# Wave 0's loads on one queue, and the weight queue asked later, in a fused attention and MLP kernel

## The chip, the cores and the metric

The kernel runs on one core of a Trainium2 chip. The core has five engines that work side by side and meet at semaphores: TensorE (PE in the profile; its weight loads are PEld), VectorE (DVE), ScalarE (ACT), GpSimd (POOL) and SyncE (SP). Transfers between memory and the core's SBUF are done by 16 DMA engines. An instruction on SP or POOL asks for a transfer; SP's transfers and POOL's are told apart in the profile as queue q1 (hardware_dynamic) and queue q0 (software_dynamic). The metric is device time in microseconds (us) for one launch, as the median of several runs.

## The reference

Four batches of eight heads, 768 tokens, head size 64. A linear attention with decay runs over blocks of 64 tokens, and its output goes through a two-layer MLP of 512 to 2048 to 512 features:

```python
for b in range(nb):
    qb, kb, vb = (q[:, :, sl], k[:, :, sl], v[:, :, sl])
    intra = np.einsum('bhic,bhjc->bhij', qb, kb) * Dmask[None]
    intra = np.einsum('bhij,bhjd->bhid', intra, vb)
    inter = np.einsum('bhid,bhde->bhie', qb * lam_pow[None], kv_state)
    out[:, :, sl] = intra + inter
    kv_state = lam_block * kv_state + np.einsum('bhsd,bhse->bhde', kb * rev_pow[None], vb)
...
h = x @ w_in
g = h * (1.0 / (1.0 + np.exp(-1.702 * h)))
return g @ w_out
```

All inputs and the output are float32. The kernel multiplies in bfloat16 and sums in float32.

## The kernel before

**Waves.** The tokens are cut into six waves (`NW`) of 128 positions in each of the four batches, 512 columns in all. Each wave goes through the attention (scores, masks, output, state), then through the MLP, and leaves 512 rows of output. The first two waves (`ND` = 2) are laid out in pairs: q, k and v of two tokens of a batch pair stand beside each other, `c` = 0 or 1 is the batch, and each `load_one` of wave 0 or 1 brings one tensor for one c: 512 KB. Wave 0 asks for it in two halves of 256 KB (four heads each), so that the first cast can start early. In the text q1, k1 and v1 are the tensors of c = 1, q0, k0 and v0 those of c = 0.

**What is done with a load.** `do_cast` (L193) multiplies k or q by a power of the decay and writes bfloat16; `g` = 0 or 1 is one half of the heads, two instructions each. `turn_pe` (L232) transposes on PE through the identity and copies back to SBUF. `d_scores` (L251) makes the scores on PE and masks them on DVE (with `split` the second half goes through an ACT copy first). `cast_v` (L223) writes v as bfloat16 in two instructions, one for each of the two interleaved tokens, and its argument says which engine takes which. `d_one` and `d_state` make the state (tile `ps_kv`), `d_out` the output (tile `ps_o`), `d_x` moves it into the MLP's input `xT`. `mlp1_half` (L406) and `mlp1` (L396) multiply by `w_in`.

**Weights.** `w_in` comes in five chunks of 2, 3, 4, 4 and 3 feature blocks of 128 (256, 384, 512, 512 and 384 KB as bfloat16), `w_out` in four chunks of 512 KB. All nine are asked on GpSimd's queue, because they are turned from float32 to bfloat16 on the way. `load_w_in(j)` and `load_w_out(j)` each issue one transfer.

**Order.** Every engine runs its instructions in the order of the program text, written out by hand under `tc.manual_schedule()`. Before it, `load(0)` asks SP for k0, q0, v0, k1 and q1, in ten halves. v1 isn't among them: GpSimd asks for it in one piece, behind `w_in` chunk 0. GpSimd's order around the change is: a copy of one element of q0's second half, which holds the engine until that half has landed (`gate_pool`, L654); `w_in` 0; v1; the cast of k1's first half; `w_in` 1; the cast of k1's second half; `w_in` 2 to 4; `w_out` 0 to 3; a mask for later waves. `gate_sync` (L637) holds SP in the same way until `w_out` 1 has landed, and then wave 1's k, q and v are asked (`load(1)`).

PE's order in wave 0's attention is: transposes of k0 and q0, scores of c = 0, state, the first half of the k1 transposes, output of c = 0, state, q1 first half, k1 second half, q1 second half, scores of c = 1, the first MLP half (`w_in` 0), state and output of c = 1, and then the rest of the MLP's first layer (`w_in` 1 to 4).

For wave 1, GpSimd casts v0 and then k1, PE transposes that k1 and goes on with the output of c = 0 (`end(1, 0)`).

Of the kernel before, what the change touches and what calls it, by code (L numbers as in the profile page):

```python
# [25 lines left out]
def kernel(  # L26
# [13 lines left out]
    nc = tc.nc  # L40
    f32 = mybir.dt.float32
    bf16 = mybir.dt.bfloat16
    B, H, S, D = q.shape
# [33 lines left out]
    loaded = {}  # L77

    def load_one(w, c, nm, src):
        x = ld.tile([P, H, 2 * D], f32, tag=f"{nm}{c}", bufs=LD_BUFS[nm], name=f"{nm}f")  # L80
        if w < ND:
            n = H if w or (nm == "v" and c) else H // 2
            for h in range(0, H, n):
                (nc.gpsimd if w == 0 and c and nm == "v" else nc.sync).dma_start(  # L84
                    out=x[:, h : h + n],
                    in_=src[2 * w + c, h : h + n, 0 : 2 * P, :].rearrange("h (s a) d -> s h (a d)", a=2))
        else:
            nc.sync.dma_start(out=x.rearrange("p h (a d) -> p (h a) d", a=2),
                              in_=src[2 * c : 2 * c + 2, :, w * P : (w + 1) * P, :].rearrange("b h s d -> s (b h) d"))
        loaded[w, c, nm] = x  # L90

    def load(w, nms="kqv"):
        src = {"k": k, "q": q, "v": v}
        if w < ND:
            for c in range(HF):
                for nm in nms:
                    if w or c == 0 or nm != "v":
                        load_one(w, c, nm, src[nm])
        else:
            for nm in nms:  # L100
                for c in range(HF):
                    load_one(w, c, nm, src[nm])
# [3 lines left out]
    ones = const.tile([1, P], f32)  # L106
    nc.vector.memset(ones, 1.0)
    load(0)

    nc.scalar.preload_act_table_set("natural_log_exp_and_others")  # L110
# [32 lines left out]
    def fill(n, new=None):  # L143
        if new:
            fill_ps[0] = acc("ps_fill", shape=[P, W], tag=new)
        for _ in range(n):
            nc.tensor.matmul(fill_ps[0], zero[:, 0:P], zero, start=True, stop=True)
# [25 lines left out]
    NCH = FFC // CW  # L173
    IN_CH = [2, 3, 4, 4, 3]
# [4 lines left out]
    def load_w_in(j):  # L179
        c0 = sum(IN_CH[:j]) * P  # L180
        nc.gpsimd.dma_start(
            out=w_in_sb[j], in_=moe_w_in.rearrange("(kc ki) f -> ki kc f", ki=P)[:, :, c0 : c0 + IN_CH[j] * P])

    def load_w_out(j):
        nc.gpsimd.dma_start(
            out=w_out_sb[j], in_=moe_w_out.rearrange("(fc fi) d -> fi fc d", fi=P)[:, j * CW : (j + 1) * CW, :])
# [6 lines left out]
    def do_cast(w, c, nm, eng, g=None):  # L193
        if g in (None, 0):
            cast[w, c, nm] = work.tile([P, 2, HD], bf16, tag=f"{nm}s{c}", bufs={"k": 2, "q": 1}[nm], name=f"{nm}s")
        f, x = loaded[w, c, nm], cast[w, c, nm]
        if w < ND:
            pw = {"k": kd_pow, "q": qd_pow}[nm]
            for R in (0, 1) if g is None else (g,):
                for j in range(2):  # L200
                    h = slice(4 * R + 2 * j, 4 * R + 2 * j + 2)
                    eng.tensor_tensor(x.rearrange("p a (r i j d) -> p r j i a d", i=2, j=2, d=D)[:, R, j],
                                      f[:, h].rearrange("p i (a d) -> p i a d", a=2),
                                      pw[:, h].unsqueeze(3).to_broadcast([P, 2, 2, D]), op=MUL)
        else:
            pw = {"k": k_pow, "q": q_pow}[nm]
            n = 2 * H // 4
            for j in range(2):
                eng.tensor_tensor(x.rearrange("p b (r i j d) -> p j (b r) i d", i=2, j=2, d=D)[:, j],  # L209
                                  f.rearrange("p h (a d) -> p (h a) d", a=2).rearrange("p (n j i) d -> p j n i d", j=2, i=2)[:, j],  # L210
                                  pw.rearrange("p b (r j i) -> p j (b r) i", i=2, j=2)[:, j].unsqueeze(3).to_broadcast([P, n, 2, D]),
                                  op=MUL)
# [10 lines left out]
    def cast_v(w, c, copies=(pool_copy, pool_copy)):  # L223
        f = loaded.pop((w, c, "v"))
        dst = v_sb[w % 2]
        if w < ND:
            for a in range(2):
                copies[a](dst[:, 2 * c + a], f.rearrange("p h (a d) -> p h a d", a=2)[:, :, a, :])
        else:
            copies[0](dst[:, 2 * c : 2 * c + 2].rearrange("p b h d -> p (b h d)"), f.rearrange("p h e -> p (h e)"))  # L230
# [20 lines left out]
    def d_scores(w, c, pp, split=False):  # L251
        kT = trans[w, c, "k"]
        s2 = [acc("ps_s") for _ in range(2)]
        for i in range(2):
            r = 2 * pp + i
            for a in range(2):
                for blk, bs in enumerate((A, Z)):
                    for h, hs in enumerate((A, Z)):
                        nc.tensor.matmul(s2[h][bs, 2 * i + a, :], kT[hs, 2 * r + a, bs], q_of(w, c, hs, r, blk),
                                         start=True, stop=True)  # L260
        for h in range(2):
            sm = work.tile([P, 2, 2, P], bf16, tag="sm", bufs=8, name="sm")
            flat = s2[h].rearrange("p (i a) s -> p i (a s)", i=2)
            if split and h:
                nc.scalar.copy(sm.rearrange("p i a s -> p i (a s)"), flat)
                flat = sm.rearrange("p i a s -> p i (a s)")
            nc.vector.tensor_tensor(sm.rearrange("p i a s -> p i (a s)"), flat,  # L267
                                    mask_d.rearrange("p o a b s -> p o (a b s)").to_broadcast([P, 2, 2 * P]), op=MUL)
            masked[w, c, pp, h] = sm
# [14 lines left out]
    def d_one(w, c, tag="a"):  # L284
        states[w, c] = t = acc("ps_kv", shape=[P, NP, D], tag=tag)
        d_state(w, c, t, A)
# [278 lines left out]
    def one_step(w, s):  # L565
# [18 lines left out]
        elif s[0] in "kq":  # L584
            do_cast(x, int(a), s[0], nc.vector)
        elif s[0] in "KQ":
            do_cast(x, int(a), s[0].lower(), nc.gpsimd)
        elif s[0] == "t":
            turn_dma(x, int(s[2]), s[1])
        elif s[0] == "v":  # L590
            cast_v(x, int(s[1]), ((act_copy, dve_copy)[s[2:] == "v"],))
        elif s[0] == "S":
            n_scores(x, int(a))
        elif s[0] == "M":
            n_masks(x, int(a))
        elif s[0] == "m":
            n_masks(x, int(a), True)
        elif s[0] == "R":
            n_rest(x)
        elif s[0] == "o":  # L600
            c11.pop(w)()
        elif s[0] == "X":
            x_sums(x)
        elif s[0] == "G":
            gate_pool(x_sum[w][3][0:1, 0, 0:1])
        elif s[0] == "g":
            m0, m1 = {"l": (0, 4), "h": (4, 8)}[s[1]]
            g_sums(w, m0, m1, tuple(int(c) - 1 for c in s[2:]))
        elif s[0] == "L":
            load(w + (1 if a == "w" else 2), "kq" if a == "k" else "v")  # L610
        else:
            raise ValueError(s)
# [20 lines left out]
    def gate_pool(x):  # L633
        nc.gpsimd.tensor_copy(behind_q, x)  # L634
# [4 lines left out]
    with tc.manual_schedule():  # L639
# [8 lines left out]
        for nm, copies in (("k", (dve_copy, act_copy)), ("q", (act_copy, dve_copy))):  # L648
            for g in range(2):
                do_cast(0, 0, nm, nc.vector, g)  # L650
            for g in range(2):
                turn_pe(0, 0, nm, copies[g], g)
                fill(2 - g if nm == "k" else 1 - g)
        gate_pool(loaded[0, 0, "q"][0:1, H // 2, 0:1])  # L654
        load_w_in(0)
        load_one(0, 1, "v", v)
        cast_v(0, 0, (act_copy, act_copy))
        d_scores(0, 0, 0)
        d_scores(0, 0, 1)
        fill(3)  # L660
        do_cast(0, 1, "k", nc.gpsimd, 0)
        load_w_in(1)
        do_cast(0, 1, "k", nc.gpsimd, 1)
        for j in range(2, len(IN_CH)):
            load_w_in(j)
        for j in range(NCH):
            load_w_out(j)
        d_one(0, 0, "mm")
        d_keep(0, 0)
        turn_pe(0, 1, "k", act_copy, 0)  # L670
# [10 lines left out]
        d_x(0, 0, 1, oz, act_copy)  # L681
        fill(1, "a")
        d_scores(0, 1, 0, True)
        cast_v(0, 1, (act_copy, dve_copy))
        nc.gpsimd.affine_select(mask, mask, pattern=[[0, 1], [1, P]], channel_multiplier=-1, base=0,
                                compare_op=mybir.AluOpType.is_ge, fill=0.0)
        gate_sync(w_out_sb[1][0:1, 0, 0:2])
        load(1)
        d_scores(0, 1, 1, True)
        mlp1_half(0, 0, 0)  # L690
# [61 lines left out]
        for i, (c, fc) in enumerate(halves):  # L752
# [8 lines left out]
            if i in (1, 2, 3, 4):  # L761
                nm = "kq"[(i - 1) % 2]
# [37 lines left out]
```

## Time and the profile before

| what | us |
|---|---|
| median of three runs | 193.56 (193.47 to 193.85) |
| the profiled execution | 193.77 |
| its span, first to last instruction | 192.1 |
| PE busy | 185.1 |
| DVE busy | 153.7 |
| ACT busy | 129.7 |
| POOL busy | 53.1 |

The times that the profile gives count from the first instruction of the span. The granted TensorE clock is 1.00 throughout. A line of the timeline reads: start, length, engine (with q where it is the engine's queue of issues), source line, operation, tiles written and read, their shapes, how many; in brackets the idle time before it and what ended it. In the transfers by queue a line gives packets, megabytes, and the time that the packets took as a share of what 16 engines have; a share above 100% means that packets overlap on an engine. The time to landing of a transfer runs from the start of its issue until the last of the 16 engines has done its part.

Two rows of transfers that the working uses, from windows around single issues:

```profile
w_in<-in_moe_w_in_dram POOLq DMA_DIRECT2D x1, 256.0 KB, 7.3
...
vf<-in_v_dram POOLq DMA_DIRECT2D x1, 512.0 KB, 7.7
```

The first was issued at 7.17 us and landed at 14.43, the second at 8.11 and landed at 15.79. The other chunks of weights landed at 17.65, 20.19, 22.73 and 24.68 (`w_in` 1 to 4) and at 27.22, 29.80, 32.30 and 34.95 (`w_out` 0 to 3). Wave 1's k0, q0 and v0 landed at 37.78, 39.24 and 40.78.

### The profile page before, as it was taken

The numbers are of one execution on the slowest core, as the hardware profiler recorded it, in microseconds if no ns is written. First come the engines' busy times: TensorE is split into PE (matmuls) and PEld (weight loads), VectorE is DVE, ScalarE is ACT, GpSimd is POOL, SyncE is SP. The second block draws the span as 40 slices with busy tenths as digits, with TensorE's granted clock in tenths as the row PEclk, the third lists the DMA queues.
The fourth block names the chain that finished last, engine by engine and source line by source line (L and its number), as shares of the span: only waits on it lengthen the run. The fifth ranks groups of instructions, "written<-read, shape, count | busy, mean of one in ns | idle before, by whom it ended". The sixth has DMA issues, their size and how long they took to land.

```text
span 192.1 us, 5543 instructions
## 1 busy us (share of the span) xinstructions
PE 185.1 (96%) x2295; PEld 152.6 (79%) x2297; DVE 153.7 (80%) x292; ACT 129.7 (68%) x242; POOL 53.1 (28%) x76
## 2 busy tenths in 40 slices
PE   7988999999999999999999999999999999999993
PEld 2556645888888887888888888888888888888882
DVE  1777689798477799979799879799889797889950
ACT  4956676257776985379896388895388875597711
POOL 5597000048467000096000295000393000000000
DMA  5999999988997799988998746999365903300113
GB/s 148 322 277 206 206 206 216 275 251 235 238 226 169 172 253 208 221 190 130 209 227 193 237 129 147 216 245 257 109 165 117 212 3 112 110 3 0 52 58 112
DMA packets 89599, 33.91 MB, mean 177 GB/s; under 512 B 67430, under 2 KB 89446, under 8 KB 89574
## 3 DMA queue, kind: packets, MB, share of 16 engines
q1 hardware_dynamic: 84676, 28.84, 60.3%
q0 software_dynamic: 4896, 4.72, 14.3%
q8 instruction: 18, 0.29, 0.7%
q14 instruction: 7, 0.06, 0.1%
q10 hardware_dynamic: 2, 0.00, 0.0%
HBM read 27.26 MB, written 6.29 MB: 175 GB/s over the span
## 4 chain that ended last, share of the span: by engine, by line
PE 80%; DVE 9%; DMA 4%; SPq 3%; issue 1%; ACT 1%; ACTq 0%
PE ps_X L461 20%; PE ps_hX L544 16%; PE ps_V L461 9%; PE ps_hV L544 8%; PE ps_h L402 5%; PE ps_h L414 5%; PE ps_Q L461 5%; PE ps_hQ L544 4%; DMA qf<-in_q_dram 4%; SPq L84 3%; DVE sm L267 2%; DVE g_s L441 2%; PE ps_s L335 2%; PE ps_o L390 2%; DVE sm L348 1%
## 5 line engine op out<-in xcount | busy, mean ns | idle before, releaser
L461 PEld LDWEIGHTS <-g_s 128*128 128x128 bf16 x384 | 36.9, 98 | 5.7 <-DVE g_s L441 0.4
L563 ACT ACTIVATE g_sb<-h_sb 128x512 bf16<-128x512 f32 x54 | 32.6, 631 | 1.2 <-DVE h_sb L552 1.2
L544 PEld LDWEIGHTS <-w_in_t 128*128 128x128 bf16 x288 | 28.2, 98 | 3.3
L461 PEld LDWEIGHTS <-g_sb 128*128 128x128 bf16 x288 | 27.4, 98 | 4.1
L221 ACT COPY part<-ps_hX 128x512 f32<-128x512 f32 x32 | 18.3, 586 | 11.5 <-PE ps_hX L544 11.5
L461 PE MATMUL ps_X<-w_out_t,g_s 128*128 128x256 bf16 x192 | 23.3, 273 | 0.2 <-DVE g_s L441 0.2
L544 PEld LDWEIGHTS <-w_in 128*128 128x128 bf16 x216 | 21.1, 98 | 2.4
L544 PE MATMUL ps_hX<-x_s,w_in_t 128*128 128x256 bf16 x144 | 21.6, 272 | 0.0
L441 DVE TENSOR_TENSOR g_s<-g_sb 128x1024 bf16<-128x1024 bf16 x24 | 16.3, 686 | 6.0 <-ACT g_sb L563 5.6
L209 POOL TENSOR_TENSOR qs<-qf,q_pow 128x512 bf16<-128x512 f32 x16 | 16.7, 1068 | 3.0 <-ACT xT L221 3.0
L209 POOL TENSOR_TENSOR ks<-kf,k_pow 128x512 bf16<-128x512 f32 x16 | 16.6, 1063 | 2.4 <-ACT qT L221 2.4
L634 POOL CAST behind_q<-x_s 1x1 f32<-1x1 bf16 x3 | 0.5, 174 | 59.7 <-DVE x_s L529 59.7
L474 ACT COPY part<-ps_X 128x512 f32<-128x512 f32 (+1 forms) x14 | 7.3, 523 | 13.1 <-PE ps_X L461 13.1
L218 DVE COPY part<-ps_hV 128x512 f32<-128x512 f32 x18 | 12.4, 688 | 4.3 <-PE ps_hV L544 4.3
L552 DVE TENSOR_TENSOR h_sb<-part,ps_hX 128x512 f32<-128x512 f32 x18 | 12.3, 681 | 2.7 <-PE ps_hX L544 2.7
L552 DVE TENSOR_TENSOR h_sb<-part,ps_hV 128x512 f32<-128x512 f32 x18 | 12.3, 683 | 1.0 <-PE ps_hV L544 1.0
L461 PE MATMUL ps_X<-w_out,g_sb 128*128 128x256 bf16 x96 | 12.6, 273 | 0.0
L461 PE MATMUL ps_Q<-w_out,g_sb 128*128 128x256 bf16 x96 | 12.5, 273 | 0.0
L552 DVE TENSOR_TENSOR h_sb<-part,ps_hQ 128x512 f32<-128x512 f32 x18 | 12.2, 679 | 0.0
L221 ACT CAST v_sb<-vf 128x1024 bf16<-128x1024 f32 (+1 forms) x13 | 11.3, 884 | 1.1 <-DMA vf<-in_v_dram 1.0
L461 PE MATMUL ps_V<-w_out_t,g_sb 128*128 128x256 bf16 x96 | 12.0, 273 | 0.0
L461 PE MATMUL ps_X<-w_out,g_s 128*128 128x256 bf16 x96 | 11.6, 272 | 0.2 <-DVE o_sb L485 0.2
(111 smaller groups left out, 358.8 us busy)
## 6 DMA issues: line engine op xcount, KB each, us to landing
kf<-in_k_dram SPq DMA_DIRECT2D x10, 512.0 KB, 6.9
qf<-in_q_dram SPq DMA_DIRECT2D x10, 512.0 KB, 6.7
vf<-in_v_dram SPq DMA_DIRECT2D x10, 512.0 KB, 6.0
out_dram<-o_sb SPq DMA_DIRECT2D x24, 128.0 KB, 2.4
out_dram<-o_sb SPq DMA_DIRECT2D x12, 256.0 KB, 2.9
w_out<-in_moe_w_out_dram POOLq DMA_DIRECT2D x4, 512.0 KB, 15.4
kf<-in_k_dram SPq DMA_DIRECT2D x4, 256.0 KB, 3.1
qf<-in_q_dram SPq DMA_DIRECT2D x4, 256.0 KB, 4.5
```

Source lines behind the costliest of these rows:

```text
L84: (nc.gpsimd if w == 0 and c and nm == "v" else nc.sync).dma_start(out=x[:, h : h + n], in_=src[2 * w + c, h : h + n, 0 : 2 * P, :].rearra ...
L209: eng.tensor_tensor(x.rearrange("p b (r i j d) -> p j (b r) i d", i=2, j=2, d=D)[:, j], f.rearrange("p h (a d) -> p (h a) d", a=2).rearran ...
L218: nc.vector.tensor_copy(out, in_)
L221: nc.scalar.copy(out, in_)
L402: nc.tensor.matmul(h, w_in_sb[j][:, kc, i * P : (i + 1) * P], xT[w][:, kc, :], start=(kc == 0), stop=(kc == KC - 1))
L414: nc.tensor.matmul(h[:, u, :], w_in_sb[j][:, kc, i * P : (i + 1) * P], xT[w][:, kc, cols], start=(kc == 0), stop=(kc == KC - 1))
L441: nc.vector.tensor_tensor(o, x, y, op=f)
L461: nc.tensor.matmul(bank[:, t], x[:, m, t * P : (t + 1) * P], y, start=(n in (1, 2, 7) and t == ts[0] * last and m == 0), stop=(m == FFC // ...
L474: nc.scalar.copy(part[w, n, t.start][:, t], bank[:, t])
L544: nc.tensor.matmul(bank[:, u], z[:, kc], y[:, kc], start=(n in (1, 2, 7) and u + kc == 0), stop=(kc == 1), skip_group_check=True)
L552: nc.vector.tensor_tensor(h, h_part[w, g, {2: 1, 5: 7, 4: 6}[n]], bank, op=ADD)
L563: nc.scalar.activation(g_of[w][:, a : b + 1 : b - a, 256 * i : 256 * i + 256], bank, GELU)
```

## The change

Three things are moved. The whole of v1 goes to SP's queue, in two halves like all the others, behind q1. GpSimd no longer waits for q0 and asks for no weights before it has cast the first half of k1: then comes `w_in` 0, then the cast of the second half, then `w_in` 1 and 2. The second instruction of the v1 cast goes from DVE to GpSimd, and `w_in` 3 and 4 and all of `w_out` are asked behind it.

```diff
     def load_one(w, c, nm, src):
...
-            n = H if w or (nm == "v" and c) else H // 2
+            n = H if w else H // 2
             for h in range(0, H, n):
-                (nc.gpsimd if w == 0 and c and nm == "v" else nc.sync).dma_start(
+                nc.sync.dma_start(
...
                 for nm in nms:
-                    if w or c == 0 or nm != "v":
-                        load_one(w, c, nm, src[nm])
+                    load_one(w, c, nm, src[nm])
...
-        gate_pool(loaded[0, 0, "q"][0:1, H // 2, 0:1])
-        load_w_in(0)
-        load_one(0, 1, "v", v)
         cast_v(0, 0, (act_copy, act_copy))
         d_scores(0, 0, 0)
         d_scores(0, 0, 1)
         fill(3)
-        do_cast(0, 1, "k", nc.gpsimd, 0)
-        load_w_in(1)
-        do_cast(0, 1, "k", nc.gpsimd, 1)
-        for j in range(2, len(IN_CH)):
-            load_w_in(j)
-        for j in range(NCH):
-            load_w_out(j)
+        for g in range(2):
+            do_cast(0, 1, "k", nc.gpsimd, g)
+            load_w_in(g)
+        load_w_in(2)
...
         d_scores(0, 1, 0, True)
-        cast_v(0, 1, (act_copy, dve_copy))
+        cast_v(0, 1, (act_copy, pool_copy))
+        for j in range(3, len(IN_CH)):
+            load_w_in(j)
+        for j in range(NCH):
+            load_w_out(j)
```

## The prediction

> **What bounds the kernel now.** The page's first part has PE busy 185.1 of 192.1 us, so time can only be won where PE stands still or is held up. I read next the chain of work that ended last, for the first 22 us, which is where the change lies.
>
> ```profile
> 6.77 7.12 DMA qf<-in_q_dram
> ...
> 13.91 0.77 DVE qs L202 x2
> 14.68 0.05 issue
> 14.72 0.40 PE ps_t L238 x4
> 15.12 0.22 PE ps_fill L147
> 15.34 0.40 PE ps_s L259 x16
> 15.74 1.06 DVE sm L267 x2
> 16.80 0.34 DVE v_sb L218
> 17.14 1.06 DVE sm L267 x2
> ...
> 18.25 0.31 PE ps_o L316 x8
> ```
>
> Columns are start, length, work. The chain enters at the second half of q of batch pair 1 (from here q1; likewise k1, v1), 256 KB that take 7.12 us from issue to landing. It then runs over DVE's cast, a transpose, the scores, the masks with DVE's half of the v1 cast between them, and ends wave 0's attention on PE at 18.55. From there to 43.56 the chain is PE alone: the MLP's 46 matmuls of L402 from 22.31, then L461. No weight wait stands on it.
>
> Then GpSimd's timeline, which holds the weight queue:
>
> ```profile
> 7.17 0.95 POOL L181 DMA_DIRECT2D w_in<-in_moe_w_in_dram  x1
> 8.11 0.92 POOL L84 DMA_DIRECT2D vf<-in_v_dram  x1
> 9.25 1.18 POOL L202 TENSOR_TENSOR ks<-kf,kd_pow 128x256 bf16<-128x256 f32 x2 [0.22 <-DMA kf<-in_k_dram]
> 10.38 0.80 POOL L181 DMA_DIRECT2D w_in<-in_moe_w_in_dram  x1
> 11.20 1.20 POOL L202 TENSOR_TENSOR ks<-kf,kd_pow 128x256 bf16<-128x256 f32 x2
> 12.34 2.29 POOL L181 DMA_DIRECT2D w_in<-in_moe_w_in_dram  x3
> ```
>
> and the transfers by queue (q1 is SP's, q0 GpSimd's; packets, MB, share) in the windows 9 to 10, 10 to 11 and 11 to 12 us:
>
> ```profile
> q1 hardware_dynamic: 685, 0.34, 113.1%
> ...
> q1 hardware_dynamic: 443, 0.22, 72.7%
> q0 software_dynamic: 119, 0.06, 44.5%
> ...
> q0 software_dynamic: 350, 0.22, 137.0%
> q1 hardware_dynamic: 11, 0.01, 6.6%
> ```
>
> The weight queue moves nothing before 10.2 us though it was asked at 7.17; it starts as SP's queue runs dry, and the last 34 packets of SP's queue then trickle until 13.9. From there to 32 us the DMA engines stay full: 207 GB/s in the window 14 to 32. Last, wave 1's start:
>
> ```profile
> 40.83 1.69 POOL L215 CAST v_sb<-vf 128x512 bf16<-128x512 f32 x2 [22.93 <-DMA vf<-in_v_dram]
> 42.48 2.33 POOL L202 TENSOR_TENSOR ks<-kf,kd_pow 128x256 bf16<-128x256 f32 x4
> ...
> 44.85 0.61 PE L238 MATMUL ps_t<-ident,ks 128*128 128x128 bf16 x8
> ```
>
> GpSimd waits for wave 1's v0, casts it, casts k1 and ends at 44.81, and PE's transposes of that k1 start at 44.85. Wave 1's loads, which come behind all weights, are thus as good as on the path.
>
> **The change, part by part.**
>
> *q1 lands earlier.* SP's 256 KB pieces land every 0.76 us (6.83, 7.59, 8.34, 9.11 by issue plus time to landing), and the first half of q1 at 10.63. At that pace the second lands at 11.4; at the latest, as now, at 13.88. Up to its first data nothing else is asked of the engines in the new order, so I take 11.4 to 12. DVE's second pair of q casts then follows the first at 13.02 rather than 13.91. PE's order puts the k1 transposes (13.64, 0.40) ahead, so the q1 transposes start at 14.04 rather than 14.72: 0.68 gained; the other 0.21 is lost behind PE.
>
> *v1's second half moves from DVE to GpSimd.* It leaves the chain: 0.34. GpSimd takes about 0.85 (half of the 1.69 above). The masks end at 18.20 - 0.68 - 0.34 = 17.18. PE is next: scores end at 15.38, then one MLP half (1.05), ps_kv (0.58) and ps_o (0.53 + 0.31) end at 17.85 against 18.56 now. So wave 0's attention gains **0.7 us**, if nothing new is late.
>
> *Removed, added, moved issues.* The gate copy (0.34), an issue of w_in (0.95) and of v1 (0.92) leave GpSimd before 9.25. They cost nothing now and gain nothing: the k1 cast there waits for k1 until 9.25 anyway. SP gets two more issues of 0.65 to 0.92 behind 7.69, done by 9.4, and its next instruction waits for w_out until 29.82: free. On GpSimd w_in 0 goes out at 10.38 (was 7.17), w_in 1 at 12.34 (10.38), w_in 2 at 13.1, then the v1 cast, then w_in 3 at about 14.9 (13.1), and the other w_in and w_out end at 19 (17.6). Behind the waiting cast stand all further weights and a mask not used before wave 2.
>
> *First weights.* SP's queue now carries 0.52 MB more, 1.5 us at 341 GB/s, so it runs dry at 12.4 instead of 10.9. The issue of w_in 0 ends at 11.18. What lies between the end of such an issue and its first data the trace bounds from above only: 10.2 - 8.1 = 2.1, with SP's queue in the way; from below it is 0. So data starts between 12.4 (no gap) and 13.3, and w_in 1 (issue ends 13.14) between 13.6 and 15.2, while w_in 0 needs 0.262/0.207 = 1.27 us. The idle gap in the weight stream is 0 to 1.9 us in all. I take about 0.85, as the middle: the start coincided with the run-out, so 2.1 overstates it. [...]
> w_in 0 took up to 4.2 us from first data (10.2) to landing (14.43), v1 and the straggling engine included; for most of its bytes the window 11 to 12 says about 1.7. It lands at 14.1 to 15.4, straggling up to 17.6 (14.43 + 3.2). PE wants it at 15.38. I take no stall.
>
> *The later weights and wave 1's loads.* The bytes ahead of each are the same as before, so they move by the gap (later) less what the straggler loses. Now one engine is 13.88 - 11.4 = 2.5 us late after the two queues met, and each chunk of weights and each of wave 1's loads is complete only when the last engine is. Without the meeting between 0 and 2.5 is won; I take 1.2, half, since SP's tail may meet w_in 0 again. Net: loads **0.35 us earlier** (1.9 later to 0.8 earlier; above that wave 0's 0.7 caps it). Slack of weights: w_out 3 lands at 34.95 and PE asks at 36.17, or 35.5 in the new order; enough unless it is 0.5 late.
>
> *What wave 1 lets through.* With its loads where they are, GpSimd still ends k1 at 44.81; PE then needs 0.55 (to 45.40), 0.53 and 0.31 and ends ps_o at 46.24, against 46.39: only 0.15 of the 0.7 passes. Loads 0.35 earlier make it 0.15 + 0.35 = **0.5**. What follows is PE's own order and DVE's, and shifts as a whole.
>
> **Sum.** 193.77 of the profiled execution (span 192.1, 1.67 around it) less 0.5 is 193.27; the runs' median is 193.56, 0.21 under that execution, so 193.06.
>
> **One more price.** The cast on GpSimd can slow DVE: g_s of L441 took 1.10 us at 40.95 beside that cast and 0.69 at 35.12 without. The new cast (13.9 to 14.8) falls between DVE's q casts and its masks of two SBUF inputs (15.7), so 0; if v1 is a microsecond late, 0.41 on the mask. [...]
>
> **Rivals.** About 0.2% (0.39 us) is what a measurement can tell from no change.
>
> 1. *It is absorbed by wave 1's loads.* The straggler's gain and the gap cancel; wave 0's 0.7 shrinks to 0.15: **193.4**. For it: 44.81 against 44.85. Against: stragglers of 2.5 us are large. 0.22.
> 2. *The weight stream starts with a hole*, slower: place, GpSimd's queue between 12.4 and 15.2. At the bound of 2.1 per issue the hole is 1.9 us and a straggler gives back 0.8: loads 1.1 later, 0.15 - 1.1 = -0.95: **194.5**; w_in 1 for PE's half at 18.5 is then late too. It decides from a hole 0.55 us larger than what the straggler gives back. For it: the engines have no hole now. Against: data came just when SP's queue was dry. 0.23.
> 3. *The v1 cast holds back w_in 3*: if v1 lands at 15.79 as it does now, the cast ends at 16.65, and w_in 3's data is ready at 16.65 + 0.76 + 2.1 = 19.5, where w_in 2 is through at 18.6: 0.9 later for all behind, 0.15 - 0.9: **194.3**. It decides from a landing at 14.9. Against: v1 is issued 0.4 earlier and on the queue that is served first. 0.10.
>
> That the change does not do what it says I leave out: the order of the issues is fixed in the code.
>
> **How the numbers follow.** Forecast (192.6 to 193.17 by itself, the low end where the whole 0.7 and some 0.3 of later waits pass): 0.45. Faster 0.45, same 0.22, slower 0.33. The range runs from 192.5 to 194.4, leaving out the far part of rival 2 and little below.
>
> **What would show it.** Right: q1's second half landing by 12, DVE's second q pair at 13.0, masks ended by 17.3, ps_o by 17.9, w_in 0 landed before 15.4, wave 1's v0 landed by 40.4, its k1 cast ended by 44.5. Wrong: q0 empty for a microsecond after SP's queue, MLP half waiting for w_in, GpSimd waiting for v1 past 14.9, wave 1's loads after 40.8.

## The result and the profile after

The changed kernel takes 194.78 us (median of 20 runs, 193.54 to 196.59) against 193.51 (20 runs, 192.77 to 195.36) for the kernel before: ratio 1.0060, 95% interval 1.0037 to 1.0084, which is 0.7 to 1.6 us slower. The profiled execution took 195.51 us with a span of 193.8; the one before had 193.77 and 192.1. The comparisons leave disturbed runs out already; for one experiment (E2) only two of six runs remain, and its profile is of one of the other four.

First the stretch in which the weights start. These are busy times by windows of one microsecond of the changed kernel; the columns are PE, PEld, DVE, ACT and POOL, then the granted clock, the busy share of the DMA engines and GB/s:

```profile
12.00:13.00 1.00, 0.50 (x20) 0.35 (x13) 1.00 (x2) 0.65 (x2) 1.00 (x2) 1.00 0.52 83
13.00:14.00 1.00, 0.87 (x14) 0.54 (x12) 1.00 (x3) 0.83 (x2) 1.00 (x3) 1.00 1.38 196
14.00:15.00 1.00, 1.00 (x37) 0.62 (x34) 0.75 (x3) 0.38 (x2) 1.00 (x2) 1.00 0.63 66
15.00:16.00 1.00, 0.36 (x14) 0.19 (x3) 1.00 (x3) 1.00 (x3) 1.00 (x3) 1.00 1.15 154
```

and the same windows of the kernel before:

```profile
12.00:13.00 1.00, 0.67 (x28) 0.55 (x27) 1.00 (x3) 0.43 (x3) 1.00 (x2) 1.00 1.12 390
13.00:14.00 1.00, 0.91 (x12) 0.59 (x12) 0.12 (x2) 0.86 (x2) 1.00 (x3) 1.00 1.16 224
14.00:15.00 1.00, 0.32 (x6) 0.28 (x5) 1.00 (x3) 0.59 (x2) 1.00 (x2) 1.00 1.29 211
15.00:16.00 1.00, 1.00 (x37) 0.53 (x35) 0.70 (x3) 0.24 (x1) 1.00 (x2) 1.00 1.27 207
```

The engines were full in every one of these windows (a share above 1); now they have two dips, 83 GB/s and 66 GB/s. The four windows moved 499 KB in all; at the 207 GB/s of the kernel before (14 to 32 us) they would move 828 KB, so about 1.6 us of stream is missing. GpSimd's timeline in the changed kernel tells why there are two:

```profile
9.67 1.18 POOL L201 TENSOR_TENSOR ks<-kf,kd_pow 128x256 bf16<-128x256 f32 x2 [6.30 <-DMA kf<-in_k_dram]
10.80 0.95 POOL L180 DMA_DIRECT2D w_in<-in_moe_w_in_dram  x1
11.76 1.39 POOL L201 TENSOR_TENSOR ks<-kf,kd_pow 128x256 bf16<-128x256 f32 x2
13.10 1.55 POOL L180 DMA_DIRECT2D w_in<-in_moe_w_in_dram  x2
14.64 0.63 POOL L214 CAST v_sb<-vf 128x512 bf16<-128x512 f32 x1
15.20 1.48 POOL L180 DMA_DIRECT2D w_in<-in_moe_w_in_dram  x2
```

The issue of `w_in` 0 ends at 11.75 and its data flows from 12.5 to 13 on. `w_in` 0 is only 256 KB and is through on 15 of the 16 engines by 14.7; `w_in` 1, whose issue ends at 13.90 behind the second k1 cast, has data from about 14.6 on. The v1 cast starts at once at 14.64: v1 had landed at 13.51.

What came of it, in the time of landing (us) by profiled execution:

| | q1, second half | `w_in` 0 | `w_in` 3 | `w_out` 1 | `w_out` 3 | wave 1's k0 |
|---|---|---|---|---|---|---|
| before | 13.88 | 14.43 | 22.73 | 29.80 | 34.95 | 37.78 |
| changed | 11.83 | 15.76 | 24.11 | 31.58 | 38.06 | 39.36 |

The stream is not back at its old rate behind the dips: from 16 to 27 us it moves 191 GB/s where the kernel before moved 206, which makes another 0.8 us. Why, the runs don't tell: with the late ask E4 has 201 and E3 187, with an early one E1 has 197 and E5 205.

PE's timeline in the changed kernel, with what ended its waits (L413 is the first part of the MLP's first layer, L460 the product with `w_out`; line numbers are one higher in the kernel before):

```profile
15.80 1.05 PE L413 MATMUL ps_h<-xT,w_in 128*128 128x256 bf16 x8 [0.64 <-DMA w_in<-in_moe_w_in_dram]
...
18.64 2.84 PE L413 MATMUL ps_h<-xT,w_in 128*128 128x256 bf16 x24
...
34.18 0.60 PE L460 MATMUL ps_X<-w_out,g_sb 128*128 128x256 bf16 x4 [0.59 <-DMA w_out<-in_moe_w_out_dram]
...
38.10 0.60 PE L460 MATMUL ps_X<-w_out,g_sb 128*128 128x256 bf16 x4 [1.57 <-DMA w_out<-in_moe_w_out_dram]
```

and the rows of the kernel before that stand against the second and the last:

```profile
19.20 2.84 PE L414 MATMUL ps_h<-xT,w_in 128*128 128x256 bf16 x24
...
36.17 0.60 PE L461 MATMUL ps_X<-w_out,g_sb 128*128 128x256 bf16 x4
```

At 18.64 PE is 0.56 us ahead of the kernel before (19.20): wave 0's attention did get faster, in spite of the wait for `w_in` 0. At 38.10 it is 1.93 us behind (36.17), having waited for `w_out` 2 and 3. The chain of waits of the changed kernel says it in two lines; the first starts with the issue on GpSimd and is mostly the queue ahead of that chunk:

```profile
18.86 19.19 DMA w_out<-in_moe_w_out_dram
...
38.10 0.60 PE ps_X L460 x4
```

In the chain before, no weight stood. From there on PE's lateness stays (ps_o of wave 1 ends at 48.32 instead of 46.39, 1.93 later), and the spans differ by 1.7. Wave 1's v0 landed at 42.4, 1.6 later too, so that GpSimd's casts alone would have held PE up nearly as much. This profiled execution is 0.7 us above the median of its kernel, and the last engine of `w_out` 3 is late even among the late asks: in E3 and E4 it landed at 37.11 and 36.44.

### The profile page after: what moved, and what is told of

It is laid out like the page before. It is cut to its first block, busy times and chain, and to the rows that moved or that the text cites. A ratio compares the mean times of both kernels' runs of the same rounds, so it can differ in the third digit from the quotient of the medians.

```text
span 193.8 us, 5549 instructions
## 1 busy us (share of the span) xinstructions
PE 183.6 (95%) x2297; PEld 150.7 (78%) x2297; DVE 154.3 (80%) x291; ACT 129.5 (67%) x242; POOL 52.5 (27%) x75
## 4 chain that ended last, share of the span: by engine, by line
PE 70%; DMA 13%; DVE 8%; POOL 5%; SPq 2%; issue 1%; ACT 1%; ACTq 0%; POOLq 0%
PE ps_X L460 19%; PE ps_hX L543 16%; DMA w_out<-in_moe_w_out_dram 10%; PE ps_V L460 9%; PE ps_hV L543 8%; PE ps_Q L460 4%; PE ps_hQ L543 4%; PE ps_h L413 4%; DMA kf<-in_k_dram 3%; DVE g_s L440 2%; POOL w_in L180 2%; PE ps_s L334 2%; PE ps_o L389 2%; SPq L84 2%; POOL ks L201 1%; DVE sm L266 1%
## 5 line engine op out<-in xcount | busy, mean ns | idle before, releaser
L460 PEld LDWEIGHTS <-g_s 128*128 128x128 bf16 x384 | 36.9, 98 | 5.7 <-DVE g_s L440 0.5
L460 PEld LDWEIGHTS <-g_sb 128*128 128x128 bf16 x288 | 27.4, 98 | 6.6 <-issue 2.5
L220 ACT COPY part<-ps_hX 128x512 f32<-128x512 f32 x32 | 18.3, 586 | 11.5 <-PE ps_hX L543 11.5
L460 PE MATMUL ps_X<-w_out_t,g_s 128*128 128x256 bf16 x192 | 23.3, 273 | 0.2 <-DVE g_s L440 0.2
L217 DVE COPY part<-ps_hV 128x512 f32<-128x512 f32 x18 | 12.4, 688 | 4.3 <-PE ps_hV L543 4.3
L460 PE MATMUL ps_X<-w_out,g_sb 128*128 128x256 bf16 x96 | 12.6, 273 | 2.2 <-DMA w_out<-in_moe_w_out_dram 2.2
L460 PE MATMUL ps_Q<-w_out,g_sb 128*128 128x256 bf16 x96 | 12.5, 273 | 0.0
L551 DVE TENSOR_TENSOR h_sb<-part,ps_hQ 128x512 f32<-128x512 f32 x18 | 12.2, 679 | 0.0
L413 PE MATMUL ps_h<-xT,w_in 128*128 128x256 bf16 x96 | 11.4, 273 | 0.6 <-DMA w_in<-in_moe_w_in_dram 0.6
L460 PE MATMUL ps_V<-w_out_t,g_sb 128*128 128x256 bf16 x96 | 12.0, 273 | 0.0
```

The costliest lines, as they stand in the source:

```text
L217: nc.vector.tensor_copy(out, in_)
L220: nc.scalar.copy(out, in_)
L413: nc.tensor.matmul(h[:, u, :], w_in_sb[j][:, kc, i * P : (i + 1) * P], xT[w][:, kc, cols], start=(kc == 0), stop=(kc == KC - 1))
L460: nc.tensor.matmul(bank[:, t], x[:, m, t * P : (t + 1) * P], y, start=(n in (1, 2, 7) and t == ts[0] * last and m == 0), stop=(m == FFC // ...
L551: nc.vector.tensor_tensor(h, h_part[w, g, {2: 1, 5: 7, 4: 6}[n]], bank, op=ADD)
```

## Experiments

Theory A: the weight queue is asked too late, the stream starts with a hole, and as the engines are busy from then on, the hole arrives at every later weight and at wave 1's loads. Rival B: the v1 cast on GpSimd holds back `w_in` 3 and what follows. Rival C: v1 on SP's queue is itself what costs.

**E1: ask early, change the rest.** (Diffs of E1 to E4 are against the changed kernel.)

```diff
+        gate_pool(loaded[0, 0, "q"][0:1, H // 2, 0:1])
+        load_w_in(0)
         cast_v(0, 0, (act_copy, act_copy))
...
             do_cast(0, 1, "k", nc.gpsimd, g)
-            load_w_in(g)
-        load_w_in(2)
+            load_w_in(g + 1)
```

> The changed kernel, with the wait for q0 and the issue of w_in 0 put back ahead of GpSimd's k1 casts (about 7.2 us), and w_in 1 and 2 one place earlier each; v1 stays on SP's queue and half of its cast on GpSimd. Theory A (the weight stream starts with a hole because the queue is asked too late, and is full from then on, so that the hole arrives at all later weights): no window of 0.5 us between 11 and 16 us under 170 GB/s, w_out 1 lands at 29.8 or before (changed kernel 31.58, before 29.80), the time returns to that of the kernel before or under it, 192.9 to 193.6. Rival B (the v1 cast on GpSimd holds back w_in 3 and what follows): stays at 194.3 to 194.8. Rival C (putting v1 on SP's queue is what costs): stays above 194.

Measured: ratio to the kernel before 1.0000 (0.9971 to 1.0029). `w_out` 1 landed at 30.01, 0.2 later than expected, and from 11 to 16 us no half microsecond was under 170 GB/s. The whole loss is gone with v1 on SP's queue and half its cast on GpSimd, even though `w_in` 3 now went out only at 16.35, behind that cast. B and C fall as explanations of the loss. It is no gain either: q1 landed at 13.47, nearly as late as before (13.88). That alone doesn't explain the missing gain: with the same early ask q1 landed at 11.62 in E12 and 11.27 in E11, and neither is clearly faster.

**E2: all weights before the v1 cast.**

```diff
-        load_w_in(2)
+        for j in range(2, len(IN_CH)):
+            load_w_in(j)
+        for j in range(NCH):
+            load_w_out(j)
...
         cast_v(0, 1, (act_copy, pool_copy))
-        for j in range(3, len(IN_CH)):
-            load_w_in(j)
-        for j in range(NCH):
-            load_w_out(j)
```

> The changed kernel, with all weights asked before the v1 cast on GpSimd instead of w_in 3 to w_out 3 behind it. Theory A (hole at the start of the weight stream): no gain, 194.4 to 195; the cast now ends near 20 us, later than PE wants it (16.8), so if anything 1 to 3 us later in wave 0's attention, which the late weights hide in part. Rival B (the cast holds back w_in 3): w_in 3 lands 0.6 us or more before the changed kernel's 24.11, and time falls to about 193.6.

Measured: 1.0178 (1.0118 to 1.0239), slower than expected. The cast starts at 18.80, and PE waits for it:

```profile
PE ps_kv L278 <- POOL v_sb L214: 2.4, 1, 2.4
```

(the columns are total, times, longest, in us). In that execution the granted clock was half as well, for 6.8 us from 19.0 on. `w_in` 3 landed 0.76 us earlier than in the changed kernel, but that is paid for several times over. How much of the loss is the wait and how much the clock, the run doesn't tell. It speaks for the place that the change gave the cast, not about the hole; E4 is the cleaner test of B.

**E3: ask still later.**

```diff
-        for g in range(2):
-            do_cast(0, 1, "k", nc.gpsimd, g)
-            load_w_in(g)
-        load_w_in(2)
+        do_cast(0, 1, "k", nc.gpsimd)
+        for j in range(3):
+            load_w_in(j)
```

> The changed kernel, with the first weights asked behind both k1 casts: w_in 0 is issued about 1.2 us later, w_in 1 0.9 us later, w_in 2 as before. Theory A: the hole grows by 0.9 to 1.2 us on w_in 0, w_out 1 lands up to 1 us after 31.58, PE waits for w_in 0 about 1.2 us longer, the time is 0.5 to 1.2 us above the changed kernel. Rival C (SP's queue is what costs): the time is within 0.3 us of the changed kernel.

Measured: 1.0096 (1.0066 to 1.0127), so 0.0036 or 0.7 us above the changed kernel, the size that A gives, though the two intervals overlap a little. The window from 13 to 14 us is nearly empty:

```profile
13.00:14.00 1.00, 1.00 (x17) 0.81 (x17) 0.62 (x3) 0.59 (x2) 1.00 (x3) 1.00 0.06 11
```

`w_in` 0 landed at 16.28 and PE waited 1.7 us in all for `w_in` instead of 0.6. `w_out` 1 landed only 0.36 us later than in the changed kernel, as `w_in` 1 went out right behind `w_in` 0.

**E4: the v1 cast back on DVE.**

```diff
-        cast_v(0, 1, (act_copy, pool_copy))
+        cast_v(0, 1, (act_copy, dve_copy))
```

> The changed kernel, with the second half of the v1 cast back on DVE; w_in 3 follows w_in 2 at once (about 14.7 rather than 15.2 us). Theory A: landings of w_in 3 and later move by less than 0.2 us and the time stays within 0.4 us of the changed kernel; masks end 0.34 us later, hidden by the wait for weights. Rival B (the cast on GpSimd holds back the weights): 0.6 us or more is won back.

Measured: 1.0042 (1.0020 to 1.0065), inside the changed kernel's interval. `w_in` 3 was issued at 14.50 and landed at 24.20 (24.11 in the changed kernel), `w_out` 1 at 31.56 (31.58): the cast holds nothing back that shows there. B expected 0.6 us or more to be won back; the timed runs show 0.0018, about 0.35 us, which is inside the noise. B falls as the cause of the loss. In this profiled execution PE waits for no weight: the clock was half from 14.06 to 17.48, and PE came to `w_out` 3 at 36.78, after its landing at 36.44.

**E5 and E12: v1 on SP's queue alone.** (The diff of E5 is against the kernel before, those of E6, E7 and E11 against E5; E12 is E5 once more.)

```diff
-            n = H if w or (nm == "v" and c) else H // 2
+            n = H if w else H // 2
...
-                (nc.gpsimd if w == 0 and c and nm == "v" else nc.sync).dma_start(
+                nc.sync.dma_start(
...
-                    if w or c == 0 or nm != "v":
-                        load_one(w, c, nm, src[nm])
+                    load_one(w, c, nm, src[nm])
...
-        load_one(0, 1, "v", v)
```

> The kernel before with one part of the change alone: v1 on SP's queue in two halves; GpSimd keeps the wait for q0, w_in 0 before the k1 casts, all other weights right behind them, and DVE keeps its half of the v1 cast. Theory A (only the late ask costs): no hole, w_out 1 lands by 30.2, and the time is that of the kernel before or up to 0.4 us under it, 192.8 to 193.4 against 193.2. Rival C (v1 on SP's queue costs): 0.5 us or more slower.

> The kernel with v1 on SP's queue alone once more, to tell its ratio of 0.998 from no change. If moving v1 is a gain by itself: again 0.996 to 0.999 of the kernel before. If the first time was chance: 0.999 to 1.002.

Measured: 0.9976 (0.9952 to 1.0000), then 0.9986 (0.9954 to 1.0018). C falls: this part costs nothing and may gain 0.1 to 0.2%, though neither interval alone shows a gain. E5 and E4 differ on GpSimd alone, that is in the gate copy and in the asks (`w_in` 0 at 7.52 or 10.67, `w_in` 1 at 10.66 or 12.97), and the ratios are 0.998 and 1.004. E5's windows:

```profile
12.00:13.00 1.00, 0.20 (x14) 0.09 (x6) 1.00 (x2) 0.64 (x2) 1.00 (x3) 1.00 1.21 282
13.00:14.00 1.00, 0.79 (x12) 0.59 (x13) 0.83 (x3) 0.35 (x1) 1.00 (x2) 0.98 1.22 299
14.00:15.00 1.00, 1.00 (x9) 0.51 (x5) 0.71 (x2) 0.72 (x2) 1.00 (x2) 0.50 1.30 215
15.00:16.00 1.00, 1.00 (x33) 0.83 (x32) 0.42 (x2) 0.25 (x1) 1.00 (x3) 0.50 1.30 197
```

The engines' share (before the last column) stays above 1.2, where the changed kernel fell to 0.52 and 0.63. `w_out` 1 landed at 29.58, wave 1's k0 at 36.11. By queue the same profile shows what fills the engines between `w_in` 0 and `w_in` 1: from 11.0 to 11.5 the weight queue has 163 packets and SP's 44, from 12.5 to 13.0 the weight queue 37 and SP's 269, v1's among them. With the late ask SP's loads are through before `w_in` 0 (v1 landed at 13.51, `w_in` 0 at 15.76), and from 14 to 15 us, at 66 GB/s, no packet of SP's queue is left to move.

**E6: ask in the middle.** E5 with the wait for q0 replaced by one for v0:

```diff
-        gate_pool(loaded[0, 0, "q"][0:1, H // 2, 0:1])
+        gate_pool(loaded[0, 0, "v"][0:1, H // 2, 0:1])
```

> The previous kernel with GpSimd's first wait on the second half of v0 in place of that of q0, so that w_in 0 is issued about 1.3 us later, at 8.5 to 8.8 us, still ahead of the k1 casts. Theory A: data of w_in 0 is ready at about 10.4, before SP's queue runs dry at 12, so there is no hole and the time is that of the previous kernel within 0.3 us; k1 casts start up to 0.5 us later. If SP's tail is disturbed less than with the early ask, q1 lands before 13 and the attention of wave 0 ends earlier, worth 0 to 0.3 us.

Measured: 1.0005 (0.9977 to 1.0033); `w_in` 0 was issued at 8.75, and its first packets came at 11.55, not at the expected 10.4. q1 landed at 11.61, v1 at 13.16, and `w_out` 1 at 29.53 (E5: 29.58): the landings show neither a hole nor a straggling tail of SP's queue. Yet no gain shows against E5.

**E7: wave 1's loads asked earlier.** E5 with:

```diff
-        gate_sync(w_out_sb[1][0:1, 0, 0:2])
+        gate_sync(w_out_sb[0][0:1, 0, 0:2])
```

> The first kernel of this group with wave 1's loads asked when w_out 0 has landed instead of w_out 1, some 2.6 us earlier. Theory A with the cap (wave 0's gain is lost on wave 1's loads, and those are late by what the weights ahead of them are late): k0 and v0 of wave 1 land up to 1 us earlier and time falls by 0.2 to 0.6 us, unless w_out 2 and 3, which then share the engines with the loads, land after PE wants them (36 us) - then it rises by as much as they are late, up to 2 us.

Measured: 1.0011 (0.9984 to 1.0038), not faster than E5. The loads were issued at 27.84 (30.46 in E5), but k0 landed at 36.52, no earlier than E5's 36.11, while `w_out` 3 slipped from 34.62 to 35.87. With the engines full (a share of 1.25 from 17 to 32 us in E5), the earlier request moved nothing forward here.

**E8: shorten GpSimd's work in wave 1.** E1 with:

```diff
-        cast_v(1, 0)
+        cast_v(1, 0, (act_copy, pool_copy))
```

> The early-ask kernel, with one of the two instructions of wave 1's v0 cast on ACT, so that GpSimd's cast of k1 in wave 1 starts about 0.85 us earlier. If wave 1's loads and GpSimd's casts behind them are what caps the gain of wave 0's attention: 0.15 to 0.5 us faster than the early-ask kernel (192.7 to 193.0). If not: within 0.2 us of it; if ACT's copies of kT and qT are delayed by the 0.6 us of the cast, slower by up to 0.3.

Measured: 1.0022 (0.9994 to 1.0050) against E1's 1.0000 (0.9971 to 1.0029): no gain. In E1 the chain of waits does come to where I had put the cap, wave 1's v0 and GpSimd:

```profile
32.00 8.29 DMA vf<-in_v_dram
40.35 1.50 POOL v_sb L214 x2
...
42.03 1.35 POOL ks L201 x3
```

From there it doesn't go into PE's transposes, though, but over GpSimd's q casts (44.36) to wave 2's loads (46.79). In the profiled execution of E8 PE's k1 transposes came at 43.52 instead of 44.28. The timed runs don't show that as time won, so the cap by GpSimd alone isn't confirmed.

**E9: `w_in` 1 asked with `w_in` 0.** Against the changed kernel:

```diff
-        for g in range(2):
-            do_cast(0, 1, "k", nc.gpsimd, g)
-            load_w_in(g)
+        do_cast(0, 1, "k", nc.gpsimd, 0)
+        load_w_in(0)
+        load_w_in(1)
+        do_cast(0, 1, "k", nc.gpsimd, 1)
         load_w_in(2)
```

> The changed kernel with w_in 1 asked right behind w_in 0, ahead of the second k1 cast. The weight stream of the changed kernel has two dips, one before the data of w_in 0 (12.3 to 13) and one before that of w_in 1 (14 to 15.5). Theory A: the second dip goes, no window of 0.5 us between 13.5 and 16 us is under 150 GB/s, w_out 1 lands 0.7 to 1.2 us before the changed kernel's 31.58, and about half of the loss comes back: 1.002 to 1.004 of the kernel before, although the second k1 cast ends 0.8 us later. Rival (only when the first weights are asked counts): no change against the changed kernel.

Measured: 1.0021 (0.9994 to 1.0049), the size that A gives, though the interval reaches from no loss to most of the changed kernel's 0.0060. The way there is only half as expected: `w_out` 1 landed 0.46 us earlier, and the second dip became a longer and shallower one instead of going (157 GB/s from 15 to 16, 117 from 16 to 17):

```profile
13.00:14.00 1.00, 0.41 (x8) 0.23 (x4) 1.00 (x2) 0.97 (x2) 1.00 (x2) 1.00 1.15 142
14.00:15.00 1.00, 0.85 (x21) 0.51 (x21) 0.88 (x3) 0.00 (x0) 1.00 (x3) 0.96 1.08 118
```

Why the queue moves only 118 to 142 GB/s there with both chunks asked, the runs don't tell.

**E10: wave 1's loads asked later.** Against the changed kernel:

```diff
-        gate_sync(w_out_sb[1][0:1, 0, 0:2])
+        gate_sync(w_out_sb[2][0:1, 0, 0:2])
```

> The changed kernel with wave 1's loads asked when w_out 2 has landed rather than w_out 1, so that they meet less of the tail of w_out 3. If the loss passes through PE's wait for w_out 3 (its last engine held up by those loads): w_out 3 lands within 2.8 us of w_out 2 (3.9 in the changed kernel), PE's wait for it shrinks by about 1 us, and the time falls by 0.3 us or more. If it passes through wave 1's loads: they land 0.5 to 1.5 us later and the time rises by as much.

Measured: 1.0052 (1.0024 to 1.0081), the changed kernel's loss. `w_out` 3 landed 2.5 us behind `w_out` 2 (3.9 in the changed kernel), and PE's wait for `w_out` fell from 2.2 to 0.4 us, as the first expectation has it; but the time stayed, and k0 of wave 1 landed at 39.33 (39.36), not later, though it was asked at 35.34 (32.46); wave 1's v1 landed at 46.93 in both. The chain of waits now enters wave 1 over these loads (k0, then v1 until 46.93). So the wait for `w_out` 3 and that for wave 1's loads look like two ends of one lateness: with the one all but gone, the chain enters through the other.

**E11: DVE rid of the cast, early ask.** E5 with both halves on ACT:

```diff
-        cast_v(0, 1, (act_copy, dve_copy))
+        cast_v(0, 1, (act_copy, act_copy))
```

> The kernel before with v1 on SP's queue alone, and both halves of the v1 cast on ACT, so that DVE's masks lose the 0.34 us of the cast and no weight waits behind a cast. If wave 0's attention counts: 0.1 to 0.3 us under the kernel with v1 on SP's queue alone, 0.995 to 0.998 of the kernel before. If wave 1's loads cap it: the same within 0.2 us. ACT's second instruction (0.6 us) delays its copy of the last scores, which may give the gain back.

Measured: 0.9992 (0.9969 to 1.0015), nothing against E5 and E12. The 0.34 us that DVE's cast takes of wave 0's chain are worth nothing that can be measured.

Taken together, by the start of the issue of `w_in` 0 in each profiled execution: 7.2 to 7.6 (E5, E11, E12, E1, E7, E8) 0.998, 0.999, 0.999, 1.000, 1.001 and 1.002; 8.75 (E6) 1.0005; 10.4 with `w_in` 1 right behind (E9) 1.002; 10.4 to 10.8 without (E4, E10, changed) 1.004, 1.005 and 1.006; 12.2 (E3) 1.010. E2 (10.6, 1.018) stands apart for its late cast. No kernel clearly beats the one before; E5 and its repeat E12 beat the changed one by 0.7 to 0.8%. That the late ask causes the loss is shown: E1 alone takes it away. Through which end it reaches the total, `w_out` 3, wave 1's loads or GpSimd's casts behind them, stays open.

## Why the prediction was wrong

I forecast 193.06 us, faster, and gave the mechanism that came about (rival 2, 194.5) a chance of 0.23.

*q1 and wave 0's attention: right.* q1's second half landed at 11.83 (taken: 11.4 to 12), the masks ended at 16.91 (17.18), and PE came to the MLP 0.56 us earlier (0.7, of which the wait of 0.64 for `w_in` 0 took part; "I take no stall" was wrong).

*The issues moved on GpSimd: right in order, 0.76 too early for `w_in` 1.* It started at 13.10 instead of 12.34: 0.42 because k1's cast started at 9.67, as its first half landed at 9.53 in this execution; 0.15 because the first issue takes 0.95 and not 0.80; 0.19 because the second cast took 1.39. At that time DVE now runs its q casts, four in 2.37 us where I had put two pairs of 0.89 and 0.77. The two beside the second k1 cast took 0.95 and 0.83, the other two 0.42 and 0.41. I weighed what DVE and GpSimd cost each other only for the v1 cast and overlooked that the earlier q casts now stand beside the k1 cast. The 0 that I took for the v1 cast stands: the mask that began beside it (14.83) took 0.69, like its counterpart before (0.69 at 15.73).

*First weights: the step that failed.* The term that was too small is the idle gap in the weight stream, taken as 0.85 us as the middle of 0 to 1.9. By the engine in the middle of the sixteen, `w_in` 2 landed 2.0 us and `w_out` 1 2.5 us later than before (20.21 against 18.20, 30.30 against 27.77). About 1.6 us of that are the two dips, and 0.8 the stream's lower rate until 27 us, which the sum did not have. The delay behind the term lay within its bounds of 0 and 2.1: from the end of an issue to its first data the changed kernel shows 0.7 to 1.1 us, E3 0.7 to 0.8 (issue ends 13.19, first packets near 13.9). The gap comes twice, since the second k1 cast lies between the first two issues and `w_in` 0 is too small to bridge it; the issues that end at 11.75 and 13.90 rather than 11.18 and 13.14 widen both.

The upper bound has a slip too: from 12.4 to 13.3 and from the end of `w_in` 0 (13.3 + 1.27) to 15.2 makes 1.5 or 1.6, not 1.9. And the reason for going to the middle, that data started just when SP's queue ran dry, doesn't hold: in E5 and E12 SP's queue holds v1 as well, and the weight queue's first packets came at 9.7 and 10.1 all the same, 1.2 and 1.6 us behind the end of the issue. The 2.1 before were thus hardly a wait for an empty queue, and in these two runs GpSimd's data was not held back until SP's was through, as the argument against rival 3 had it.

*The straggler: the sign right, the size too large.* The last engine was 2.03 us behind the middle one at `w_out` 1 before and 1.27 after: 0.76 won, where I took 1.2. Net, the weights came 1.8 us later (31.58 against 29.80) instead of 0.35 earlier, and wave 1's loads 1.6.

*The slack of weights: overrun.* `w_out` 3 was to be late only from 0.5 us on; it landed 3.1 us later, 38.06. Its last engine met wave 1's loads, too; with those asked later (E10) it landed at 36.97, but in E4, with the loads asked as in the changed kernel, at 36.44, so that how much they add isn't shown.

*The cap by wave 1.* Its loads are late, k0 by 1.6 us, but E8 doesn't confirm that GpSimd's casts behind them set the price.

*Rival 3* had the cast wait for v1 until 15.79; v1 was there at 13.51, and E4 shows no cost clear of noise.

## What to carry to other kernels

Here the weight queue fed a long stretch with all transfer engines full (a share of 1.22 from 16 to 27 us), and what was missing at its start wasn't made up later: every weight from `w_in` 3 on landed 1.3 us or more behind its old time, and PE waited for the stream's last chunks, 20 us on. When requests are moved behind compute on the issuing engine, lay out for every request when its issue ends, when its data can flow and when the request ahead runs dry, and add all the gaps; the small first request covered little here (`w_in` 0, 256 KB, was through on 15 of the 16 engines by 14.7, and from 14 to 15 us 66 GB/s moved). A gain in front of such a stream can be lost behind it: here PE was 0.56 us ahead at 18.64 and 1.93 behind at 38.10.

## What was not expected of the hardware

The granted TensorE clock fell to half for some 3.4 us in part of the executions: in E5's windows above it is 0.50 from 14 us on, and it is full again at 17.4. The profiles of E4 and E9 have such a stretch too, that of E2 one of 6.8 us; the changed kernel's has none before its last microsecond. In E5 it comes behind a window in which PE is busy 0.20 of a microsecond (12 to 13 us). That alone doesn't decide it: in E1 the same window has 0.23, and the clock stays full. What sets it off, the runs don't tell. Nine of the changed kernel's 20 timed runs have a mean clock of 0.991 or less, as such a stretch leaves it (0.989 in the profiled executions of E4, E5 and E9), and eleven have 0.998 or 1.000; in 29 runs of the kernel before, beside E1, there were two of the former. It isn't the main cause of the result: the changed kernel's runs at 0.998 or above have a mean of 194.6 us against 193.2 for those 29 less two, and its other nine 195.2.
